# Sliding-window attention and an MLP mixer on one core: the float32 loads of q on ScalarE's DMA queue, with new order lists

## The chip, the core and the metric

The kernel runs on one core of a Trainium2 chip. The core has five engines that run side by side, each in its own program order: TensorE (PE, matrix multiplies), VectorE (DVE), ScalarE (ACT), GpSimd (POOL) and SyncE (SP, which here only issues DMAs). They tell each other what is done by semaphores. DMAs are issued by an engine and carried out by DMA engines. TensorE writes into PSUM banks, from which VectorE or ScalarE copy the result into SBUF.

The metric is the device time of one execution in microseconds (us). Lower is better.

## The reference

Attention with a window of 128 and a linear bias over 8 batches of 8 heads, then a mixer over tokens and over channels (batch 8, sequence 576, head size 64, model width 512, token width 256, channel width 1536):

```python
scores = (1/8) * q @ k^T                  # per batch and head, 576 x 576
rel = pos[:, None] - pos[None, :]
scores = where((0 <= rel) & (rel < 128), scores - slope[h] * |rel|, -1e9)
attn = softmax(scores)
x = (attn @ v)                            # to batch x 576 x 512
h = relu(x^T @ w_tok1) @ w_tok2
u = x + h^T
out = u + relu(u @ w_ch1) @ w_ch2
```

The inputs and the output are float32; the matrix multiplies are done in bfloat16.

## The kernel before

The 576 tokens of a batch are four blocks of 128 and a tail of 64. A batch passes through these steps, each a small function that emits instructions, and each with a short name in the order lists. The digit is a block or a pair of heads (hp); a mark ' means the next batch, '' the one after.

- Loads: `v` (values), `l` and `q` (k and q of a pair of heads, of batches 0 and 1), `qt` (their tails), `Lk`, `Lq` (k and q of batches 2 to 7), `LW` (`W1`, `W1t`, `W2` of the token mixer), `G0` to `G2` (the three column groups of `WC1`, one group for four `C`), `H0`, `H1` (the two halves of `WC2`). All of these are issued by GpSimd, which casts to bfloat16 on the way, except `l0`, `q0`, `l1`, `q1` of batch 0: these are float32 loads through SyncE's queue (`load_f32`), and `ck0`, `cq0`, `ck1`, `cq1` cast them, k on ScalarE and q on VectorE.
- Transposes of q and k: for batches 0 and 1 on TensorE (`A0` to `A3`, `AT` for the tail), with copies out of PSUM that the tuples `AQ_ACT` and `AK_DVE` give to ScalarE or VectorE; for later batches by DMA (`Zq`, `Zk`).
- Scores: `S<kb><j>` for key block kb and head group j, then exp on ScalarE, then a multiply by the mask on VectorE. Batch 0 adds its bias on TensorE, and its first two scores are halves (`s0`, `t0` and so on).
- Probabilities times values: `P0` to `P4`; for batch 0 by pairs of heads, `p0` to `p3`.
- Token mixer: `K0`, `K1` (first product and relu), `U0` to `U3` and `UT` (second product and the sum with x); for batch 0 `k0` to `k3` and `u0` to `u3`.
- Transposes of u: `X0` to `X3`; for batches 0 to 2 on TensorE, for batches 3 to 7 by DMA from `X0` and `X2` (`U_DMA`). For batch 0, `x0` to `x3`.
- Channel mixer: `C0` to `C11` (first product, relu into `r2`, on VectorE for the members of `DVE_RELU`, else on ScalarE), `D<c><part>` (second product of block c in three parts, sum, store). Two batches share the tail: `T0` to `T2` and `E0` to `E2`. `Y` transposes the tail of u by DMA.
- Others: `W1` to `W4` are so many matrix multiplies of zeros that keep TensorE busy; `I`, `J`, `B` make the identity, the distances and the bias; `O`, `e1`, `e2`, `ek`, `ex`, `FC` are memsets on GpSimd; `M`, `m` make the masks; `LC` copies a constant.

Five lists hold the order in which these names are emitted: `PROLOGUE` and `FIRST` for batch 0, `SECOND` for batch 1, `PERIOD` for each of batches 2 to 6, and `LAST` for batch 7. The order of a list is the program order on every engine at once, so it sets which work fills an engine while another result is awaited, and the order of each DMA queue. `PERIOD` works on `C`, `D` of its batch, on `P`, `K`, `U`, `X` of the next and on `S` of the one after.

PSUM holds two double banks for scores and `P` (`psS`, taken in turn by `S2`), three banks for nearly all else (`psM`, taken in turn by `M`), and one for tails and zeros (`psT`). A step that takes a bank waits until the bank's last content has been copied out. The taking in turn:

```python
def S2():
    t = psS[srot[0] % 2]
    srot[0] += 1
    return t
def M():
    t = psM[mrot[0] % 3]
    mrot[0] += 1
    return t
```

Other tuples: `U_ACT` (the sum of `u` by an identity multiply on TensorE and a copy on ScalarE; else the sum on VectorE), `X_DVE` and `x_DVE` (copies of `X` and `x` on VectorE), `k_DVE` (relu of `k` on VectorE), `SPLIT` and `S_M` (scores of batch 0 with two exps, and in `psM`).

Of the kernel before, what the change touches and what calls it, by code (L numbers as in the profile page):

```python
# [16 lines left out]
CH2_PARTS = 3  # L17
MASK_LATER = 1
U_DMA = (3, 4, 5, 6, 7)
U_ACT = (0, 1, 2, 3)  # L20
X_DVE = (0, 1, 2)
K_DVE = (0,)
PROLOGUE = """
W4 O J I W3 l0 B W3 ck0 q0 l1 q1 l23 FC cq0 W1 q23 v4 A0 qt v2 v0 W3 ck1 cq1 s1 A1 v1 S00 t1 S20
W2 A3 v3 LW A2 AT S11 l01' S30 q01' ek ex S21 M3 p0 l23' LC q23' G0 p1 M1 S01 k0 S31 u0 p2 M2 k1
p3 qt' G1 M0 A1' A0' m0 W2 A2' u1 v2' e1 A3' e2 v4' S00'
"""
FIRST = """
G2 v3' k3 v1' x0 v0' H1 m1 H0 k2 S20' x1 W2 AT' u3 u2 Lk'' Lq'' UT Zq'' x3 Zk'' x2 S10' Lk'''
S31' v0''' C5 v4'' S30' S01' v3'' v0'' C11 C8 C9 S21' S11' E2 C3 C10 C4 Lq''' v1'' v2'' P4' C1  # L30
C7 v4''' E0 C2 C6 P2' C0 P0' P3' D00 v2''' P1' D01 D02 K0' K1' D10 D11 U1' D12 Zq''' U2' X1' U3'
U0' Zk''' D20 D30 D21 E1 D31 X2' UT' D22 S00'' D32 T0' X0'
"""
SECOND = """
Lk''' X3 S31' S30' C8 C7 S20' v1'' C5 S11' S01' C9 v1''' C11 C2 v3'' T1 P0' C3 Lq''' C1 C4 S10'
S21' T2 C10 C0 C6 v0''' P4' v2''' P1' D00 v3''' D01 P3' P2' D02 K0' K1' S20'' S01'' D10 D11 D12
U1' UT' U0' U2' v4''' U3' X0' S21'' S11'' D20 D21 X3' S10'' S00'' E0 E1 D22 E2 X2' D30 X1' D31
D32 P0''
"""
PERIOD = """  # L40
C7 Zq'' C3 S30' S31' C8 Zk'' C11 C6 Y C1 T0 P2' P4' T1 C4 C2 Lk''' P1' C10 C9 T2 P3' C0 C5 K0'
S01'' S00'' K1' D00 v3''' v4''' D01 Lq''' D02 U2' U0' UT' U3' v1''' U1' P0'' D20 v2''' D21 D10
v0''' X2' X3' X1' X0' D22 S10'' S11'' D30 D11 D31 D12 E0 S20'' S21'' D32 E1 E2
"""
LAST = """
C3 C0 C2 C8 T0 C9 C1 C5 T2 C4 C6 Y C11 T1 C7 C10 D00 E0 E1 D01 D02 D10 D11 E2 D20 D12 D21 D30
D22 D31 D32
"""
VROW = 96
NPB = 9  # L50
SPLIT = (0, 1, 3, 5, 6)
S_M = (2, 4, 5, 6)
S_P = ()
Y_DMA = (3, 5, 7)
x_DVE = (1, 3)
k_DVE = ()
AK_DVE = (0, 1, 2, 4, 6, 7)
AQ_ACT = (1, 2, 3, 4, 5, 6, 7)
DVE_RELU = (4, 5, 7, 8, 10)


@with_exitstack
def kernel(
# [57 lines left out]
    qf0 = T("qf0", [P, 4, 4 * D], f32)  # L121
    kf0 = T("kf0", [P, 4, 4 * D], f32)
# [593 lines left out]
    def tok2_hp(hp):  # L716
        def f():
            t = M()
            hc = slice(hp * P, (hp + 1) * P)
            for c in range(NC):  # L720
                for j in range(2):
                    nc.tensor.matmul(t[:, c * P:(c + 1) * P], lhsT=W2[:, j, c * P:(c + 1) * P],
                                     rhs=r1[0][:, j, hc], start=(c == 0 and j == 0),
                                     stop=(c == NC - 1 and j == 1 and hp not in U_ACT))
# [87 lines left out]
    def fill_x1():  # L812
        nc.gpsimd.memset(xt[1][:, :], 0.0)

    def load_f32(dst, src, hp):
        hs = slice(2 * hp, 2 * hp + 2)
        nc.sync.dma_start(out=dst[:, hs, :],
                          in_=src[0, hs, 0:SM, :].rearrange("h (p j) d -> p h (j d)", j=4))

    def cast_f32(cp, dst, src, hp):  # L820
# [9 lines left out]
    def names(b):  # L830

        d = {}
        for kb in range(NC):
            for j in range(2):
                d[f"S{kb}{j}"] = score(b, kb, j)
        for qb in range(NC):
            d[f"P{qb}"] = pv(b, qb)
        d["P4"] = pv_tail(b)
        for i in range(2):
            d[f"K{i}"] = tok1(b, i)  # L840
        for c in range(NC):
            d[f"U{c}"] = tok2(b, c)
            d[f"X{c}"] = utrans(b, c)
        d["UT"] = tok2_tail(b)
        for ht in range(NHT):
            d[f"C{ht}"] = ch1(b, ht)
        if b % 2:
            for g in range(3):
                d[f"T{g}"] = ch1_tail(b, g)
            if b in Y_DMA:  # L850
                d["Y"] = utail_trans(b)
        for c in range(NC):
            for i, f in enumerate(ch2(b, c, CH2_PARTS)):
                d[f"D{c}{i}"] = f
        if b % 2:
            for i, f in enumerate(ch2_tail(b, CH2_PARTS)):
                d[f"E{i}"] = f
        for c in range(NC + 1):
            d[f"v{c}"] = lambda c=c: load_v(b, c)
        if b >= PE_BATCHES:  # L860
            d["Lq"], d["Lk"] = lambda: load_tokens(qn, qnt, q, b), lambda: load_tokens(kn, knt, k, b)
            d["Zq"] = lambda: dma_transpose(qT[b % 2], qn, qnt)
            d["Zk"] = lambda: dma_transpose(kT[b % 2], kn, knt)
        else:
            for nm, dst, src in (("q", qs, q), ("l", ks, k)):
                for hp in range(NHP):
                    d[f"{nm}{hp}"] = lambda dst=dst, src=src, hp=hp: load4(dst, src, b, hp)
                for hp in (0, 2):
                    d[f"{nm}{hp}{hp + 1}"] = lambda dst=dst, src=src, hp=hp: load4(dst, src, b, hp, 4)
            d["qt"] = lambda: load_qk_tail(b)  # L870
            for hp in range(NHP):
                d[f"A{hp}"] = pe_transpose(b, hp)
            d["AT"] = pe_transpose_tail(b)
        if b == 0:
            for hp in range(NHP):
                d[f"M{hp}"] = lambda hp=hp: mask_exps(hp)
                d[f"p{hp}"] = pv_hp(hp)
                d[f"k{hp}"] = tok1_hp(hp)
                d[f"u{hp}"] = tok2_hp(hp)
                d[f"x{hp}"] = utrans_hp(hp)  # L880
            for hp in range(2):
                d[f"q{hp}"] = lambda hp=hp: load_f32(qf0, q, hp)
                d[f"l{hp}"] = lambda hp=hp: load_f32(kf0, k, hp)
                d[f"cq{hp}"] = lambda hp=hp: cast_f32(nc.vector.tensor_copy, qs, qf0, hp)
                d[f"ck{hp}"] = lambda hp=hp: cast_f32(nc.scalar.copy, ks, kf0, hp)
            d["LC"] = late_constants
            d["FC"] = first_constants
            d["e1"], d["e2"] = lambda: ones_v(1), lambda: ones_v(2)
            d["ek"], d["ex"] = fill_k1, fill_x1
# [62 lines left out]
```

## Time and profile before

| | |
|---|---|
| median of 5 runs | 293.05 us (292.74 to 294.53) |
| the profiled execution | 292.99 us, of which its span is 290.9 us |
| granted TensorE clock | 1.00 in every stretch |
| instructions in the profile | 6132 |
| loads and stores | 38.38 MB, mean 132 GB/s |
| issues of the float32 loads, per load | 256 KB, 0.45 us on SyncE, 3.6 us (k) and 3.8 us (q) to landing |

How to read it: the span runs from the first to the last instruction; the profiled execution's time is a little longer. Busy time of an engine is the union of its instructions. TensorE's multiplies are pipelined, so that a row's duration (379 ns for 512 columns) is longer than its distance to the next (0.22 us). A chain of waits leads back from the last instruction, at each step to what released it. In the timeline a bracket holds the idle time ahead of an instruction and what ended it. SPq and POOLq are the sequencers' entries, in which a DMA is issued.

### The profile page before, as it was taken

To read this page: it belongs to the slowest core of one execution; us is meant where nothing else is said; L and a number is where in the kernel's file an instruction comes from. 1 tells how busy PE (TensorE), PEld (TensorE's weight loads), DVE (VectorE), ACT (ScalarE), POOL (GpSimd) and SP (SyncE) were. 2 spreads that over 40 slices of the span, in tenths; PEclk is the share of its full clock that TensorE was granted. 3 is DMA by queue.
4 is the path that set the end of the run, shared out by engine and by line. 5 is a ranking of instruction groups with operands and counts; after the bars stand their busy time and mean duration, and the time that the engine had idled before them with its cause. 6 is when DMAs were issued, how large, how long until landed. Compare 5 with 4: busy or idle time off the path is not lost.

```text
span 290.9 us, 6132 instructions
## 1 busy us (share of the span) xinstructions
PE 280.0 (96%) x2531; PEld 155.9 (54%) x2552; DVE 157.0 (54%) x310; ACT 124.9 (43%) x195; POOL 103.6 (36%) x140
## 2 busy tenths in 40 slices
PE   8898999999999999999999999998999999999995
PEld 3476646554574555544664455543664456545543
DVE  4246676547467557646637457646637467522222
ACT  3897962028715452326441552326441552104300
POOL 8996743079339605920294004920000000000000
PEclk9999999999999999999999999999999999999999
DMA  7999999799999999999899577999603620042014
GB/s 169 147 186 197 181 206 155 145 166 140 168 167 175 160 226 82 136 152 229 106 130 162 131 156 106 139 156 182 146 0 87 96 72 2 36 110 90 0 50 132
DMA packets 150267, 38.38 MB, mean 132 GB/s; under 512 B 137440, under 2 KB 145760, under 8 KB 150240
## 3 DMA queue, kind: packets, MB, share of 16 engines
q0 software_dynamic: 103152, 17.41, 79.0%
q1 hardware_dynamic: 47088, 20.59, 32.2%
q8 instruction: 20, 0.33, 0.5%
q14 instruction: 7, 0.06, 0.0%
HBM read 35.85 MB, written 9.44 MB: 156 GB/s over the span
## 4 chain that ended last, share of the span: by engine, by line
PE 84%; DMA 6%; POOL 5%; ACT 2%; issue 2%; DVE 1%; POOLq 0%; ACTq 0%
PE psM L548 29%; PE psM L607 25%; PE psM L481 4%; PE psM L506 4%; PE psT L565 4%; PE psM L629 4%; PE psS L356 3%; DMA utb<-ub 3%; DMA qs<-in_q_dram 3%; PE psS L420 2%; PE psS L416 2%; POOL vp L190 1%; PE psS L448 1%; ACT pe L370 1%; PE psM L588 1%
## 5 line engine op out<-in xcount | busy, mean ns | idle before, releaser
L548 PE MATMUL psM<-utb,WC 128*128 128x512 bf16 x384 | 89.4, 379 | 2.0 <-DMA utb<-ub 1.2
L607 PE MATMUL psM<-WC,r 128*128 128x512 bf16 x353 | 84.8, 379 | 0.9
L370 ACT ACTIVATE pe<-psS 128x1024 bf16<-128x1024 f32 x56 | 54.5, 1025 | 42.1 <-PE psS L356 41.8
L548 PEld LDWEIGHTS <-WC 128*128 128x128 bf16 x384 | 35.3, 98 | 41.0 <-issue 3.6
L554 ACT ACTIVATE r<-psM 128x512 bf16<-128x512 f32 x56 | 33.3, 599 | 54.5 <-PE psM L548 54.5
L607 PEld LDWEIGHTS <-r 128*128 128x128 bf16 x372 | 34.3, 98 | 40.8 <-issue 3.8
L190 POOL DMA_DIRECT2D kn<-in_k_dram x24 | 21.0, 889 | 76.8 <-DMA kT<-kn 75.5
L376 DVE TENSOR_TENSOR pb<-pe,masks 128x1024 bf16<-128x1024 bf16 x42 | 29.0, 690 | 27.2 <-ACT pe L370 27.2
L612 DVE TENSOR_TENSOR ob<-psM,ub 128x512 f32<-128x512 f32 x31 | 21.4, 690 | 28.3 <-PE psM L607 26.6
L551 DVE TENSOR_SCALAR r<-psM 128x512 bf16<-128x512 f32 x40 | 27.4, 688 | 16.2 <-PE psM L548 15.9
L190 POOL DMA_DIRECT2D vp<-in_v_dram x32 | 29.1, 947 | 1.8 <-DMA WC<-in_moe_w_ch_dram 1.6
L190 POOL DMA_DIRECT2D qn<-in_q_dram x24 | 21.3, 936 | 6.3 <-DMA WC<-in_moe_w_ch_dram 5.8
L430 DVE TENSOR_TENSOR xb<-psS,rt 128x512 bf16<-128x512 f32 x28 | 19.4, 692 | 1.0
L508 DVE TENSOR_TENSOR ub<-psM,xb 128x512 bf16<-128x512 f32 x28 | 17.5, 682 | 1.5 <-PE psM L506 1.5
L420 PE MATMUL psS<-vp,pb 128*128 128x65 bf16 x224 | 15.7, 193 | 0.0
L420 PEld LDWEIGHTS <-pb 128*128 128x128 bf16 x224 | 13.6, 97 | 3.1
L429 DVE RECIPROCAL rt<-psS 128x8 f32<-128x8 f32 x28 | 5.7, 204 | 17.0 <-PE psS L420 17.0
L506 PE MATMUL psM<-r,W 128*128 128x512 bf16 x56 | 14.5, 379 | 0.0
L356 PE MATMUL psS<-qT,kT 64*128 64x256 bf16 x168 | 13.3, 272 | 0.5 <-ACT pe L370 0.5
L481 PE MATMUL psM<-xb,W 128*128 128x256 bf16 x112 | 13.4, 273 | 0.0
L416 PE MATMUL psS<-vp,pb 128*128 128x65 bf16 x168 | 12.8, 193 | 0.0
L565 PEld LDWEIGHTS <-WC 128*128 128x128 bf16 x192 | 11.6, 98 | 2.3 <-issue 0.2
(131 smaller groups left out, 300.4 us busy)
## 6 DMA issues: line engine op xcount, KB each, us to landing
out_dram<-ob SPq DMA_DIRECT2D x31, 256.0 KB, 2.4
vp<-in_v_dram POOLq DMA_DIRECT2D x32, 128.0 KB, 5.6
kn<-in_k_dram POOLq DMA_DIRECT2D x24, 128.0 KB, 4.4
qn<-in_q_dram POOLq DMA_DIRECT2D x24, 128.0 KB, 4.8
WC<-in_moe_w_ch_dram POOLq DMA_DIRECT2D x3, 512.0 KB, 10.3
WC<-in_moe_w_ch_dram POOLq DMA_DIRECT2D x2, 768.0 KB, 12.6
out_dram<-ob SPq DMA_DIRECT2D x10, 128.0 KB, 2.4
ks<-in_k_dram POOLq DMA_DIRECT2D x3, 256.0 KB, 6.1
```

The costliest lines, as they stand in the source:

```text
L190: nc.gpsimd.dma_start(out=dst, in_=src[b, :, c * P:(c + 1) * P, :].rearrange("h s d -> s h d"))
L356: nc.tensor.matmul(s[h][:, a * 256:(a + 1) * 256], lhsT=kT[i][r, kb, hp, :], rhs=qT[i][r, kb:kb + 2, hp, :], start=True, stop=True)
L370: nc.scalar.activation(out=e[:, h, :], in_=s[n][:, None, :] if split else t2[:, :, :], func=ACT.Exp, scale=scale)
L376: nc.vector.tensor_tensor(out=p[:, :].rearrange("p (h x) -> p h x", h=2), in0=e[:, :, :], in1=masks[:, j].rearrange("p h g a x -> p h (g a ...
L420: nc.tensor.matmul(ov, lhsT=prob(b, qb, h, 0), rhs=vt[:, qb, h, 0:D + 1], start=first, stop=(hh == 3))
L481: nc.tensor.matmul(st["t"][h][:, dh * 256:(dh + 1) * 256], lhsT=W1[:, c, dh * P:(dh + 1) * P], rhs=by_half(xb[b % 2][:, c, :])[:, h], star ...
L506: nc.tensor.matmul(t[:, :], lhsT=W2[:, j, c * P:(c + 1) * P], rhs=r1[b % 2][:, j, :], start=(j == 0), stop=(j == 1))
L548: nc.tensor.matmul(t[:, :], lhsT=WC1[:, cb, ht * P:(ht + 1) * P], rhs=utb[b % 2][:, :, cb, :], start=(cb == 0), stop=(cb == NCB - 1))
L551: nc.vector.tensor_scalar(out=r2[b % 2][:, ht, :], in0=t[:, :], scalar1=0.0, scalar2=None, op0=ALU.max)
L554: nc.scalar.activation(out=r2[b % 2][:, ht, :], in_=t[:, :], func=ACT.Relu)
L565: nc.tensor.matmul(psT[:, j * P:(j + 1) * P], lhsT=WC1[:, cb, ht * P:(ht + 1) * P], rhs=utt[pi2][:, cb, :, :], start=(j == 0 and cb == 0), ...
L607: nc.tensor.matmul(t[:, :], lhsT=r2[b % 2][:, ht, c * P:(c + 1) * P], rhs=WC2[:, ht, :], start=(ht == 0), stop=(ht == NHT - 1))
```

## The change

`load_f32` gets the queue as an argument: q's two float32 loads are issued by ScalarE, k's two stay on SyncE. All five order lists are different, and eight tuples that say which engine copies what. No step is added or taken away; only u0 of batch 0, which leaves `U_ACT`, loses four identity multiplies on TensorE and is added on VectorE instead.

```diff
-U_ACT = (0, 1, 2, 3)
-X_DVE = (0, 1, 2)
+U_ACT = (1, 2, 3)
+X_DVE = (0, 2)
 PROLOGUE = """
-W4 O J I W3 l0 B W3 ck0 q0 l1 q1 l23 FC cq0 W1 q23 v4 A0 qt v2 v0 W3 ck1 cq1 s1 A1 v1 S00 t1 S20
-W2 A3 v3 LW A2 AT S11 l01' S30 q01' ek ex S21 M3 p0 l23' LC q23' G0 p1 M1 S01 k0 S31 u0 p2 M2 k1
-p3 qt' G1 M0 A1' A0' m0 W2 A2' u1 v2' e1 A3' e2 v4' S00'
+l0 q0 l1 q1 W4 I J W3 B O ck0 W3 l23 q23 FC W1 cq0 v4 qt A0 cq1 v0 v2 W3 ck1 s1 A1 S00 t1 v1 S20
+v3 W2 A2 A3 AT q01' S11 LW S30 l23' W2 ex ek l01' S21 p0 M1 q23' G0 LC p1 M2 S01 k0 S31 u0 p3 M3
+k1 p2 qt' G1 v4' M0 A1' A0' m1 u1 m0 A2' S10'
 """
 FIRST = """
-G2 v3' k3 v1' x0 v0' H1 m1 H0 k2 S20' x1 W2 AT' u3 u2 Lk'' Lq'' UT Zq'' x3 Zk'' x2 S10' Lk'''
-S31' v0''' C5 v4'' S30' S01' v3'' v0'' C11 C8 C9 S21' S11' E2 C3 C10 C4 Lq''' v1'' v2'' P4' C1
-C7 v4''' E0 C2 C6 P2' C0 P0' P3' D00 v2''' P1' D01 D02 K0' K1' D10 D11 U1' D12 Zq''' U2' X1' U3'
-U0' Zk''' D20 D30 D21 E1 D31 X2' UT' D22 S00'' D32 T0' X0'
+A3' v3' e2 k3 G2 v1' v2' v0' k2 x0 S00' H0 e1 H1 S20' AT' W2 u3 u2 UT Lk'' x1 Lq'' Zq'' x3 Zk''
+Lk''' v0''' x2 S30' v0'' C5 v3'' v1'' S01' E2 S31' C11 C8 C9 S21' S11' C3 C4 C10 Lq''' v2'' P4'
+C1 v4'' C7 C0 P2' C2 C6 v4''' P0' v2''' P3' D00 E0 D01 P1' D02 K0' K1' D10 D11 U1' D12 X1' Zq'''
+U3' U0' U2' D20 D21 D30 X2' UT' Zk''' D31 S00'' D22 S20'' D32 E1 T0' X0'
 """
 SECOND = """
-Lk''' X3 S31' S30' C8 C7 S20' v1'' C5 S11' S01' C9 v1''' C11 C2 v3'' T1 P0' C3 Lq''' C1 C4 S10'
-S21' T2 C10 C0 C6 v0''' P4' v2''' P1' D00 v3''' D01 P3' P2' D02 K0' K1' S20'' S01'' D10 D11 D12
-U1' UT' U0' U2' v4''' U3' X0' S21'' S11'' D20 D21 X3' S10'' S00'' E0 E1 D22 E2 X2' D30 X1' D31
-D32 P0''
+X3 S31' S30' C8 Lk''' v0''' C5 S01' T1 v2''' S11' C11 C7 C3 C6 P0' C4 S10' S21' v3'' v1''' C0 T2
+C9 v3''' C1 C10 P4' v1'' C2 P1' Lq''' D00 D01 P3' P2' D02 K0' K1' S20'' S01'' D10 D11 D12 U1'
+UT' U0' U2' v4''' U3' X0' S21'' S11'' D20 D21 X3' S00'' S10'' D22 E0 E1 E2 X2' D30 D31 X1' D32
+P0''
 """
 PERIOD = """
-C7 Zq'' C3 S30' S31' C8 Zk'' C11 C6 Y C1 T0 P2' P4' T1 C4 C2 Lk''' P1' C10 C9 T2 P3' C0 C5 K0'
-S01'' S00'' K1' D00 v3''' v4''' D01 Lq''' D02 U2' U0' UT' U3' v1''' U1' P0'' D20 v2''' D21 D10
-v0''' X2' X3' X1' X0' D22 S10'' S11'' D30 D11 D31 D12 E0 S20'' S21'' D32 E1 E2
+Zq'' C11 C3 C7 S31' S30' C8 Zk'' Y P2' C1 C6 C4 C9 C10 T0 P4' C0 P1' C2 Lk''' T1 P3' C5 T2 K0'
+K1' S01'' Lq''' v4''' S00'' D00 D01 D02 U2' U0' v3''' UT' U3' U1' v0''' v1''' P0'' D20 X1' v2'''
+D10 D21 X2' X0' D22 S10'' X3' S11'' D11 D30 D31 D12 E0 S21'' S20'' D32 E1 E2
 """
 LAST = """
-C3 C0 C2 C8 T0 C9 C1 C5 T2 C4 C6 Y C11 T1 C7 C10 D00 E0 E1 D01 D02 D10 D11 E2 D20 D12 D21 D30
-D22 D31 D32
+C10 C4 C5 T2 C2 C7 C8 C3 T0 C6 C11 T1 C0 C1 C9 D00 E0 D01 E1 Y D02 D10 D11 E2 D12 D30 D20 D31
+D21 D22 D32
 """
-SPLIT = (0, 1, 3, 5, 6)
+SPLIT = (1, 3, 4, 5)
-x_DVE = (1, 3)
-k_DVE = ()
-AK_DVE = (0, 1, 2, 4, 6, 7)
-AQ_ACT = (1, 2, 3, 4, 5, 6, 7)
-DVE_RELU = (4, 5, 7, 8, 10)
+x_DVE = (0, 1, 2)
+k_DVE = (1,)
+AK_DVE = (1, 2, 4, 6)
+AQ_ACT = (2, 4, 5, 6)
+DVE_RELU = (3, 5, 7, 10, 11)
...
-    def load_f32(dst, src, hp):
+    def load_f32(queue, dst, src, hp):
         hs = slice(2 * hp, 2 * hp + 2)
-        nc.sync.dma_start(out=dst[:, hs, :],
+        queue.dma_start(out=dst[:, hs, :],
                           in_=src[0, hs, 0:SM, :].rearrange("h (p j) d -> p h (j d)", j=4))
...
-                d[f"q{hp}"] = lambda hp=hp: load_f32(qf0, q, hp)
-                d[f"l{hp}"] = lambda hp=hp: load_f32(kf0, k, hp)
+                d[f"q{hp}"] = lambda hp=hp: load_f32(nc.scalar, qf0, q, hp)
+                d[f"l{hp}"] = lambda hp=hp: load_f32(nc.sync, kf0, k, hp)
```

## The prediction

> **What bounds the kernel now.** I read the page first, then the stretches of the span as a table, then what TensorE waits for in the first 36 us, then the chain of waits and the timelines around those waits. From the page:
>
> ```profile
> PE 280.0 (96%) x2531; PEld 155.9 (54%) x2552; DVE 157.0 (54%) x310; ACT 124.9 (43%) x195; POOL 103.6 (36%) x140
> PE 84%; DMA 6%; POOL 5%; ACT 2%; issue 2%; DVE 1%; POOLq 0%; ACTq 0%
> ```
>
> TensorE is busy for 280.0 of 290.9 us, and the chain lies on it for 84%. An order can only win back the 10.9 us in which it is idle. Where they are, by stretch (first number after the times: width, second: TensorE busy):
>
> ```profile
> 0.00:11.30 11.30, 9.76 (x73) 4.12 (x73) 3.87 (x16) 6.68 (x13) 10.25 (x24) 1.00 1.05 161
> 11.30:22.60 11.30, 10.48 (x206) 8.29 (x206) 5.08 (x15) 10.18 (x27) 11.20 (x18) 1.00 1.64 176
> 22.60:35.70 13.10, 11.46 (x202) 8.40 (x202) 7.83 (x21) 11.11 (x21) 8.72 (x13) 1.00 1.64 188
> ...
> 132.90:166.00 33.10, 32.74 (x297) 18.55 (x300) 18.37 (x35) 13.61 (x20) 12.57 (x15) 1.00 1.28 147
> 166.00:198.80 32.80, 31.51 (x255) 16.31 (x257) 20.56 (x38) 13.91 (x19) 12.57 (x15) 1.00 1.40 146
> 198.80:232.00 33.20, 33.07 (x299) 18.72 (x302) 17.76 (x34) 13.52 (x20) 0.00 (x0) 1.00 0.50 94
> 262.00:291.00 29.00, 25.34 (x164) 13.94 (x164) 7.23 (x12) 5.97 (x10) 0.00 (x0) 1.00 0.22 68
> ```
>
> The first 35.7 us hold 1.54 + 0.82 + 1.64 = 4.0 us of idle TensorE, the end 3.7 (its last result on the way out), the iterations between 0.1 to 1.3 each. In the first 35.7 us ScalarE is nearly full as well (10.18 of 11.30, 11.11 of 13.10). What TensorE waits for there (us, times, longest), and the chain at the same place (start, us):
>
> ```profile
> PE psM L234 <- DMA qs<-in_q_dram: 1.2, 2, 0.7
> PE psS L356 <- ACT pe L370: 0.5, 1, 0.5
> PE psM L234 <- ACT qT L239: 0.5, 2, 0.2
> PE psM L722 <- ACT r L713: 0.4, 1, 0.4
> 17.31 7.98 DMA qs<-in_q_dram
> ```
>
> Loads of q set the pace twice: at 11.30 (q23) and at 25.34 (q23', issued at 17.31). The queue's rate over the first 30 us, in 40 slices, levels off near 200 GB/s from 16 us on: the loads stand behind one another.
>
> ```profile
> GB/s 0 0 53 280 352 223 258 206 148 164 145 158 135 153 146 150 148 170 124 148 178 175 175 195 191 187 195 195 196 197 208 201 203 207 183 173 201 203 197 174
> ```
>
> Where the queue edit acts, in the timelines (start, us):
>
> ```profile
> 0.80 1.28 ACT L822 ACT_TABLE_LOAD   x1 [0.80 <-PEq L936]
> 1.33 0.45 SPq L817 DMA_DIRECT2D qf<-in_q_dram  x1
> 3.64 1.26 DVE L791 TENSOR_SCALAR sid<-ident 128x128 bf16<-128x128 bf16 x8 [0.22 <-POOL ident L776]
> 4.64 0.52 DVE L822 CAST qs<-qf 128x512 bf16<-128x512 f32 x1
> 1.06 4.61 PE L750 MATMUL psT<-zt 128*128 128x512 bf16 x11 [1.06 <-DVE zt L745]
> 5.60 0.41 PE L234 MATMUL psM<-ident,qs 128*64 128x128 bf16 x8
> ```
>
> The first cast of q starts when VectorE is through with `sid` (line 791), not when q lands, and TensorE is filled with 11 warm-up matmuls until about 5.5 us.
>
> **What the Trainium skill says.** "DMA: Bandwidth & Descriptors", section "Issuing engines are not separate DMA queues": loads issued from several engines run on the same 16 DMA engines and interleave; only the issuing time is saved. The trace agrees as far as it goes: one issue on SP takes 0.45 us, the rate afterwards is common to all. "ScalarE: Activation LUTs", "What ACT_TABLE_LOAD costs": the load proper takes 1283 ns; the trace has 1.28 us, and it now stands behind two issues. "TensorE: Matmul & The Clock Gate", "What's actually happening": the array starts at half clock and needs about 3.4 us of work. That fits the 11 warm-up matmuls, which fill 4.6 us and of which the change keeps all.
>
> **The change part by part.** Durations are those of the profiled execution: span 290.9, time 292.99, so 2.09 lie around the span; the median of the runs is 293.05, 0.06 more.
>
> 1. Queue of q. Two issues leave SP and go ahead of the table load on ScalarE: 2 x 0.45 = 0.9 us, so the table is in at about 0.80 + 0.9 + 1.28 = 3.0 us. The first cast of k on ScalarE starts at 3.70 and waited 1.6 us for its load: the issues are hidden. Without that cover they cost 0.9. q's first piece is issued at 0.8 in place of 1.33, but then shares the engines with k's, so I take the landing as unchanged to 0.5 earlier. I, J before O bring `ident` forward by over 1 us, so `sid` and the cast end sooner; next late is the warm-up: the last starts at 5.29 and takes 0.21, floor 5.50. Gain 0.1.
> 2. q23 is issued before FC (four memsets, 4.46 to 5.42): 0.94 us earlier. It can land 0 to 0.9 earlier, since the engines are busy; I take 0.4. The transposes A2, A3 start at 11.30 minus 0.45, floor 10.21 + 0.43 - 0.1 = 10.55.
> 3. Copies shifted by the tuples: VectorE instead of ScalarE for u0, the relu of k1, x0 and x2 (x3 to ScalarE), and two of the q copies of hp 3; one k copy goes back. Net four ScalarE instructions of about 0.59 less, 2.4 us in 10 to 35 us, and as much more on VectorE, which has 5.1 of 11.3 and 7.8 of 13.1 busy: cover enough. Without u0's four identity matmuls TensorE saves 4 x 0.056 = 0.2.
> 4. The loads reordered: before LW, l01', q01', l23', q23'; after q01', LW, l23', l01', q23'. A load of 256 KB takes 256 KB / 195 GB/s = 1.34 us of queue. The weights come 1.34 later: W2 landed at 13.53 + 5.5 = 19.0 (its issue, and the time to landing in the view of its tile, as for all landings here), now 19.0 + 1.34 - 0.4 = 19.95. u0 started at 20.18: no loss, but its floor. The transposes A1' started at 22.58 and need l01', now third: third place landed (l23', 16.58 + 8.0) at 24.58, of which 1.5 look like stragglers, as second place landed at 14.99 + 6.7 = 21.7 and 21.7 + 1.34 = 23.0. Less 0.4: between 22.6 and 24.2; I take 23.2, a loss of 0.6 there.
> 5. From A1' to C11. Before: 22.58 to 35.66, 13.1 us, in which the warm-up W2 is 0.43, the wait for q23' 0.89 (24.45 to 25.34) and ScalarE waits 0.27 + 0.24 + 0.67. After: W2 stands before S21, u1 lies under the wait for q23', and the score blocks are spread as S30' C5 S01' S31'. I take away 0.43, 0.89 and half of the 1.18, and give back 0.8 for u1 and A2', which now wait for the copies of A1' on ScalarE (0.5 each). 12.0 us. C11 begins at 23.2 + 12.0 = 35.2, 0.45 before the old 35.66. Floor: C11 needs G2, landed at 24.83 + 10.3 = 35.1, less 0.4.
> 6. FIRST and SECOND, 36 to 99 us: the wait of 0.5 at 56 us, where X1' needs the bank of D12, goes over to U3', which takes that bank now. Nothing.
> 7. PERIOD, five times 33 us. Zq'' moves ahead of two C, S01'' and S00'' behind K1', Lq''' together with Lk''', and other relus go to VectorE. SP's sequence of stores and transposes is the same instruction for instruction, POOL's the same loads in another order, and as many changes between full and half array (93 against 92). Between the transposes X0' and the next C lies the same work, so the waits of 0.85 (132 us) and 1.3 (197 us) for `utb` stay. Nothing, bounds -0.2 to +0.4 an iteration.
> 8. LAST: another order of the same C; the last two pieces, D22 and D32, are as before. Nothing.
>
> Sum: -0.45, span 290.45, time 292.5.
>
> **The rivals.** *Loads first.* Both halves of q and k land 0.9 sooner, l01' is in at 22.6, C11 reaches its floor near 34.7 (-0.95), and half of the 2.2 us of `utb` waits goes because the iterations' loads drain sooner: 292.99 - 0.95 - 1.1 = 290.9. For it: 4.0 us are there to be had. Against it: the rate in the stretch of loads is flat. *l01' late.* It lands at 24.6 with the stragglers: C11 at 36.6, +0.95: 293.9. For it: that place in the queue did so before. *P2' too early (the slower side).* In PERIOD, P2' now comes right after C8; before, C8, C11, C6 and C1 stood between. It takes the score bank of S31', whose exp lasts 1.03 and starts about 0.2 after the matmuls, while only S30' (0.54) and C8 (0.86) lie between: a margin of 0.2 us. It decides once ScalarE starts that exp more than 0.2 late; at 0.4 a time, five iterations, +2.0: 295.0. Against it: C11, C3, C7 ahead of it all have their relu on VectorE. *No effect*: the edits shift waits within the load-bound start; that is my forecast with -0.45 as a size.
>
> **How the numbers follow.** This measurement can tell about 0.5% (1.46 us) from no change. Forecast 292.5, chance 0.45; loads first 290.9, 0.24; l01' late 293.9, 0.14; P2' 295.0, 0.17. Faster by over 0.5% (under 291.6): most of the second and a little of the first, 0.27. Slower (over 294.5): most of the last and some of the third, 0.22. Rest 0.51. The range from 290.9 to 294.8 leaves out the further half of the two outer cases. The forecast's own range is 291.7 to 293.4.
>
> **What would show it.** Right: A2 at 10.6 to 11.1; A1' waiting for `ks` and starting at 22.6 to 24.2; no wait for `qs` at A2'; C11 at 34.8 to 35.7; the iterations at 33.1 on average; both `utb` waits still there. Wrong: TensorE waiting for ScalarE or VectorE at P2' (line 416) in every iteration; W1 or W2 awaited at k0 or u0; the iterations' `utb` waits gone or doubled.

## The result, and the profile after

| | before | after |
|---|---|---|
| median of all runs | 294.13 us (80 runs) | 293.49 us (43 runs) |
| ratio after / before, run side by side | | 0.9961, 95% [0.9945, 0.9978] |
| the profiled execution | 292.99 us, span 290.9 | 293.13 us, span 291.1 |

The change makes the kernel faster by 0.39%, between 0.22 and 0.55%; of the 293.05 us that stand for before ahead of the prediction, that is 1.1 us (0.6 to 1.6). The ratio leaves out executions that fell into a slower state, while the medians are over all of them, so that their quotient, 0.998, is another number. The forecast was 0.45 us, within 0.5%: the right side, and a little under the measured range. The two profiled executions do not show the gain: the one of after is even 0.14 us longer, and the one of before is among the shorter ones (15 of its 80 are shorter still). So the first question is where a gain sits that one pair of traces hides.

The page of after (busy time by engine, the chain, and the queue that is new):

```profile
PE 280.6 (96%) x2527; PEld 155.8 (54%) x2548; DVE 158.7 (55%) x312; ACT 124.7 (43%) x192; POOL 103.3 (35%) x140
PE 82%; DMA 9%; POOL 5%; issue 1%; ACT 1%; DVE 1%; POOLq 0%; ACTq 0%
q10 hardware_dynamic: 544, 0.52, 0.5%
```

TensorE runs four instructions less (u0's identity multiplies), ScalarE three less, VectorE two more. The chain now lies more on DMA (9% for 6%). The stretches, cut at the same events as those of before (A2; A1'; C11; then the same times):

```profile
0.00:10.52 10.52, 9.46 (x72) 4.07 (x72) 4.08 (x16) 6.11 (x11) 9.51 (x23) 1.00 1.09 174
10.52:23.13 12.61, 10.98 (x203) 8.16 (x202) 6.05 (x17) 10.15 (x26) 11.65 (x18) 1.00 1.51 164
23.13:34.85 11.72, 11.21 (x201) 8.68 (x199) 8.49 (x23) 10.13 (x18) 8.41 (x13) 1.00 1.60 191
...
132.90:166.00 33.10, 32.97 (x298) 18.62 (x301) 18.33 (x34) 13.45 (x20) 12.58 (x15) 1.00 1.29 146
166.00:198.80 32.80, 31.43 (x255) 16.23 (x255) 20.89 (x39) 13.78 (x19) 12.58 (x15) 1.00 1.36 147
198.80:232.00 33.20, 33.05 (x298) 18.65 (x301) 17.91 (x34) 13.47 (x20) 0.00 (x0) 1.00 0.42 90
262.00:291.00 29.00, 25.51 (x165) 14.04 (x164) 7.40 (x12) 5.97 (x10) 0.00 (x0) 1.00 0.23 69
```

The way to C11 is 34.85 us long instead of 35.7: the first stretch is 0.8 shorter, the second 1.3 longer, the third 1.4 shorter. From 132.9 us on, TensorE's busy time is that of before within 0.3 us. What TensorE waits for in the first 36 us (us, times, longest), and the chain there (start, us):

```profile
PE psM L704 <- DMA W<-in_moe_w_tok_dram: 1.2, 1, 1.2
...
PE psM L548 <- DMA WC<-in_moe_w_ch_dram: 0.2, 1, 0.2
```

```profile
12.16 6.71 DMA W<-in_moe_w_tok_dram
...
24.02 10.79 DMA WC<-in_moe_w_ch_dram
...
34.85 2.76 PE psM L548 x12
```

Both waits for q (1.2 us before) and the waits for ScalarE are gone. In their place stands one wait for the first half of the token weights (k0, line 704), which landed at 12.16 + 6.71 = 18.87 us, and a short one for the last column group of `WC1` (C11, line 548).

How far the work has come in the two traces, in us from the start of the span:

| | A0 | A2 | k0 | A1' | C11 | first C of batch 2 | of batch 3 | of batch 5 | of batch 7 | last result of TensorE |
|---|---|---|---|---|---|---|---|---|---|---|
| before | 5.60 | 11.30 | 18.28 | 22.58 | 35.66 | 102.76 | 133.16 | 198.83 | 261.26 | 287.45 |
| after | 5.39 | 10.52 | 18.91 | 23.13 | 34.85 | 102.33 | 132.92 | 198.84 | 261.43 | 287.61 |

The lead of 0.8 us at C11 is 0.4 at 102 us, 0.2 at 133 and gone at 199. Two things take it: the lists behind C11, and two waits for `utb`, the transposed u, near 132 and 197 us.

The lists first. In the 14 traces of this case (before, after and the twelve experiments below) the way between milestones depends on the list alone, to 0.02 us, once the two waits are taken off:

| us | old list (5 traces) | new list (9 traces) |
|---|---|---|
| C11 to the first C of batch 2 (`FIRST`, `SECOND`) | 67.11 | 67.48 |
| first C of batch 2 to that of batch 7, less the two waits (`PERIOD`, five times) | 156.34 | 156.72 |
| first C of batch 7 to the last result of TensorE (`LAST`) | 26.18 | 26.18 |

So the new lists give back 0.37 + 0.38 = 0.75 us of what the start gains. In `FIRST`, 0.11 of it is a longer wait for a bank (0.46 us at U3' for 0.35 at X1'); the rest there was not traced. In `PERIOD` the cause can be seen at P2' (line 416), which now stands right behind C8 (line 548) and takes the score bank that the exp of S31' (line 370) still reads. First after, then before, where more C stand between (start, us):

```profile
136.05 1.94 ACT L370 ACTIVATE pe<-psS 128x1024 bf16<-128x1024 f32 x2 [3.08 <-PE psS L365]
136.17 1.04 PE L548 MATMUL psM<-utb,WC 128*128 128x512 bf16 x4
137.12 0.19 PE L416 MATMUL psS<-vp,pb 128*128 128x65 bf16 x1
```

```profile
141.74 1.89 PE L548 MATMUL psM<-utb,WC 128*128 128x512 bf16 x8
143.46 0.19 PE L416 MATMUL psS<-vp,pb 128*128 128x65 bf16 x1
```

At their usual distance of 0.216 us the four matmuls of C8 make room for P2' at 137.03; it starts at 137.12, 0.05 after the first of the two exps is through (136.05 + 1.02). In before it starts as soon as the matmuls ahead of it make room (141.74 + 8 x 0.215). The same 0.08 us stands in each of the five iterations of all nine traces with the new `PERIOD`, each time 51 to 52 ns behind the end of that exp, and in none with the old one: 0.4 us in five. In the list of waits it is missing, since that counts idle time from the modelled end of the matmul before, which lies later than its turn.

Then the waits. In after they are the two for `utb` that before has:

```profile
PE psM L548 <- DMA utb<-ub: 1.2, 1, 1.2
PE psM L548 <- DVE pb L376: 0.8, 1, 0.8
```

The second is put down to VectorE, which had long been done; the second transpose of u, issued at 124.7 us and 8.1 on its way, landed at 132.8, and C started at 132.9. Counted as the gap less the usual distance of two matmuls, the two waits are 0.97 and 1.41 us in after, 0.85 and 1.32 in before, 0.2 us more. With that the account of the pair closes: -0.81 at C11, +0.37, +0.38 and +0.21 make +0.15, and the last result comes at 287.61 for 287.45. Such a wait ends with a transfer, not with TensorE. The issues of the transfers for 132 us followed TensorE's lead (123.3 and 124.7 us in after, 123.6 and 125.0 in before), but their time on the way, 7.8 to 8.7 us, differs by more than the lead. So a lead that TensorE brings there can be lost or can grow.

### The profile page after: what moved, and what is told of

It is laid out like the page before. It is cut to its first block, busy times and chain, and to the rows that moved or that the text cites. A ratio compares the mean times of both kernels' runs of the same rounds, so it can differ in the third digit from the quotient of the medians.

```text
span 291.1 us, 6139 instructions
## 1 busy us (share of the span) xinstructions
PE 280.6 (96%) x2527; PEld 155.8 (54%) x2548; DVE 158.7 (55%) x312; ACT 124.7 (43%) x192; POOL 103.3 (35%) x140
## 4 chain that ended last, share of the span: by engine, by line
PE 82%; DMA 9%; POOL 5%; issue 1%; ACT 1%; DVE 1%; POOLq 0%; ACTq 0%
PE psM L548 29%; PE psM L607 25%; PE psM L506 4%; PE psM L481 4%; PE psT L565 4%; DMA WC<-in_moe_w_ch_dram 4%; PE psM L629 4%; DMA utb<-ub 3%; PE psS L356 3%; PE psS L420 2%; DMA W<-in_moe_w_tok_dram 2%; PE psS L416 2%; POOL vp L190 1%; PE psS L448 1%; POOL qkt L193 1%
## 5 line engine op out<-in xcount | busy, mean ns | idle before, releaser
L554 ACT ACTIVATE r<-psM 128x512 bf16<-128x512 f32 x56 | 33.5, 599 | 36.6 <-PE psM L548 36.6
L499 ACT ACTIVATE r<-psM 128x512 bf16<-128x512 f32 x7 | 4.2, 598 | 22.4 <-PE psM L490 22.4
```

The source lines that it names most:

```text
L554: nc.scalar.activation(out=r2[b % 2][:, ht, :], in_=t[:, :], func=ACT.Relu)
```

## The experiments

Each ratio is to the kernel before, run side by side on the same chip, with its 95% interval. The runs e1 to e4, e5 to e8 and e9 to e12 are of three chips, on which before had medians of 293.09, 294.07 and 293.21 us, so medians are compared within such a group only. "C11" and "waits" (the two for `utb`, near 132 and 197 us) are of the profiled execution.

### The queue and the parts

**e1_queue_alone**: before, with q on ScalarE's queue and the four loads at the head of the list (`load_f32` takes the queue as in the change; "..." marks what is left out).

```diff
-W4 O J I W3 l0 B W3 ck0 q0 l1 q1 l23 FC cq0 W1 q23 v4 A0 qt v2 v0 W3 ck1 cq1 s1 A1 v1 S00 t1 S20
+l0 q0 l1 q1 W4 O J I W3 B W3 ck0 l23 FC cq0 W1 q23 v4 A0 qt v2 v0 W3 ck1 cq1 s1 A1 v1 S00 t1 S20
...
-                d[f"q{hp}"] = lambda hp=hp: load_f32(qf0, q, hp)
+                d[f"q{hp}"] = lambda hp=hp: load_f32(nc.scalar, qf0, q, hp)
```

> The kernel before with nothing changed but the queue: the four float32 loads are issued first, q's on ScalarE and k's on SyncE; all else in the old order. If the gain (about 0.4%, 1.1 us) comes from the start's order, this gives 0 to 0.3 us less than before: the first transposes at 5.4 to 5.5 in place of 5.60, q23 still awaited until about 11.0 to 11.3. If the second queue is the cause, it gives about 1 us less than before, with q23 in before 10.6.

Measured: 0.9987 [0.9962, 1.0012]; C11 35.22; waits 0.62 and 1.37. A2 came at 11.41 us, no earlier than in before, though q23 was in at 10.77. The middle of the ratio is 0.4 us less; the "about 1 us" of a queue that is the cause lies at the end of the interval.

**e2_queue_undone**: after, with q back on SyncE's queue.

```diff
-                d[f"q{hp}"] = lambda hp=hp: load_f32(nc.scalar, qf0, q, hp)
+                d[f"q{hp}"] = lambda hp=hp: load_f32(nc.sync, qf0, q, hp)
```

> The changed kernel with all four float32 loads on SyncE's queue again, in the order k, q, k, q. If the order of the start is the cause, it stays within 0.3 us of the changed kernel, with A2 at 10.5 to 10.9 and k0 waiting for W1 until about 19. If the second queue is the cause, it falls back to the time of the kernel before.

Measured: 0.9971 [0.9946, 0.9995]; C11 34.54; waits 1.46 and 1.36. C11 comes as early as with two queues, so the lists bring it forward without the second queue. At 102 us this run led before by 0.73 us; at 133.10 by 0.06, after a wait for `utb` of 1.46.

**e3_start_alone** and **e4_period_alone**: e3 is after with the `PERIOD`, the `LAST` and (from batch 2 on) the relu tuple of before; e4 is before with those of after.

```diff
...
-            if ht in DVE_RELU:
+            if ht in (DVE_RELU if b < 2 else DVE_RELU_LATER):
```

> The changed kernel's PROLOGUE, FIRST, SECOND and tuples with the old PERIOD and LAST (and the old relu engines from batch 2 on). If the start is the cause: ratio to before about 0.996, as the whole change; the first C of batch 1's successors (102.8 before) about 0.4 sooner. If the new PERIOD is the cause: 1.000.

Measured: 0.9990 [0.9965, 1.0015]; C11 34.55; waits 1.00 and 0.57. The first C of batch 2 came at 102.03, 0.73 us sooner than in before, and still the ratio is not the 0.996 expected of a start that is the cause.

> The old PROLOGUE, FIRST, SECOND and tuples with the changed PERIOD and LAST (and the new relu engines from batch 2 on). If the start is the cause: ratio 1.000, within 0.1%. If the new PERIOD is the cause: about 0.996, with the waits for the transposed u at 132 and 197 us shorter than 0.85 and 1.3. If P2' right after C8 costs a wait, slower than before by up to 0.4 an iteration.

Measured: 0.9993 [0.9969, 1.0017]; C11 35.61; waits 0 and 1.47.

What follows from the four: all lists together without the queue (e2) are faster than before, by 0.05 to 0.54%; the queue, the start and the period alone can't be told from nothing. The start moves C11 forward in e2 and e3, the new period (e4) doesn't, and the waits for `utb` are between 0 and 1.5 us whatever the lists. The two parts, 0.1% each at their middle, don't add up to 0.39%, but their intervals are wide enough for it.

### Where the start now waits

**e5_weights_first**: after, with the token weights ahead of q01' and l01' ahead of l23', the order of the loads in before.

```diff
-v3 W2 A2 A3 AT q01' S11 LW S30 l23' W2 ex ek l01' S21 p0 M1 q23' G0 LC p1 M2 S01 k0 S31 u0 p3 M3
+v3 W2 A2 A3 AT LW S11 q01' S30 l01' W2 ex ek l23' S21 p0 M1 q23' G0 LC p1 M2 S01 k0 S31 u0 p3 M3
```

> The changed kernel with the loads of batch 1 and the token mixer's weights in an order near the old one (LW, q01', l01', l23', q23'). Theory: the wait of 1.3 us for W1 ahead of k0 goes (k0 at about 17.6, A1' at about 22.0), but C11 still needs G2, whose place in the queue is the same, so it starts at 34.5 to 34.8 as in the changed kernel (34.85) and the time stays within 0.3 us of it. Rival: the wait for W1 is what limits the start; then C11 comes about 1 us sooner, at 33.9, and the time falls by as much.

Measured: 0.9968 [0.9945, 0.9991]; k0 at 17.73 for 18.91, A1' at 21.86 for 23.13, C11 at 35.37 for 34.85; waits for `utb` 0.30 and 1.73. What TensorE waits for in the first 36 us of this run:

```profile
PE psM L548 <- DMA WC<-in_moe_w_ch_dram: 1.3, 1, 1.3
...
PE psM L234 <- DMA qs<-in_q_dram: 0.8, 1, 0.8
PE psM L722 <- DMA W<-in_moe_w_tok_dram: 0.4, 1, 0.4
```

The wait at k0 goes and A1' follows it 1.3 us forward. What the wait at k0 alone was worth, e5 doesn't tell: in after l01' landed at 23.31 us and A1' took it up at 23.38, so without the wait at k0 A1' would have met that load, and e5 moved both forward. Then the time is waited for again: for q23', and for the last group of `WC1`. C11 came 0.5 us later than in after, where it was expected as early or up to 0.35 earlier, and the ratio is that of after within the intervals. The start is bound by the loads in a row; here the load moved forward handed the wait to the next.

### The two waits for u

In before and in after the loads of a batch (k, q, v by GpSimd) begin when the DMA transposes of q and k have freed their source. They then still run when SyncE issues the transposes of u at the end of the iteration. **e6_z_early** takes after and issues `Zq`, `Zk` one stage earlier, behind D22 (in `SECOND` behind X2') instead of at the head of the next iteration; `Lq` of batch 4 goes right behind its `Lk`.

```diff
-X3 S31' S30' C8 Lk''' v0''' C5 S01' T1 v2''' S11' C11 C7 C3 C6 P0' C4 S10' S21' v3'' v1''' C0 T2
+X3 S31' S30' C8 Lk''' Lq''' v0''' C5 S01' T1 v2''' S11' C11 C7 C3 C6 P0' C4 S10' S21' v3'' v1''' C0 T2
-C9 v3''' C1 C10 P4' v1'' C2 P1' Lq''' D00 D01 P3' P2' D02 K0' K1' S20'' S01'' D10 D11 D12 U1'
+C9 v3''' C1 C10 P4' v1'' C2 P1' D00 D01 P3' P2' D02 K0' K1' S20'' S01'' D10 D11 D12 U1'
-UT' U0' U2' v4''' U3' X0' S21'' S11'' D20 D21 X3' S00'' S10'' D22 E0 E1 E2 X2' D30 D31 X1' D32
+UT' U0' U2' v4''' U3' X0' S21'' S11'' D20 D21 X3' S00'' S10'' D22 E0 E1 E2 X2' Zq''' Zk''' D30 D31 X1' D32
-Zq'' C11 C3 C7 S31' S30' C8 Zk'' Y P2' C1 C6 C4 C9 C10 T0 P4' C0 P1' C2 Lk''' T1 P3' C5 T2 K0'
+C11 C3 C7 S31' S30' C8 Y P2' C1 C6 C4 C9 C10 T0 P4' C0 P1' C2 Lk''' T1 P3' C5 T2 K0'
-D10 D21 X2' X0' D22 S10'' X3' S11'' D11 D30 D31 D12 E0 S21'' S20'' D32 E1 E2
+D10 D21 X2' X0' D22 Zq''' Zk''' S10'' X3' S11'' D11 D30 D31 D12 E0 S21'' S20'' D32 E1 E2
```

> The changed kernel with the DMA transposes of q and k (Zq, Zk) of batches 4 to 7 issued one stage earlier (after E2 in SECOND, after D22 in PERIOD), and Lq of batch 4 right after its Lk. Theory: the two waits for the transposed u (about 1.0 at 132 us and 1.4 at 197 us) come from loads that are still draining under those transposes, and they swallow what the start gains. With the loads released 3 to 6 us sooner the wait at 197 goes to under 0.4 and the one at 132 to under 0.5: 1.2 to 2.4 us less than before's ratio of 0.996, thus 0.988 to 0.992. Rival: the waits are the transposes' own length (3 to 4 us each) or the early transposes block SP's stores: no gain, or slower with TensorE waiting for the stores' buffers.

Measured: 0.9924 [0.9895, 0.9954], median 291.15 (expected were 0.988 to 0.992); no wait for `utb` in the profiled execution. GpSimd's timeline, after and then e6 (start, us, then the load of k of batch 7; in the bracket how long GpSimd was idle before, and what ended it):

```profile
178.56 3.50 POOL L190 DMA_DIRECT2D kn<-in_k_dram  x4 [22.84 <-DMA kT<-kn]
```

```profile
167.67 3.51 POOL L190 DMA_DIRECT2D kn<-in_k_dram  x4 [17.81 <-DMA kT<-kn]
```

GpSimd waits for the transpose `kT<-kn` both times; in e6 that ends 10.9 us sooner. The two transposes of u that end near 197 us, after and then e6, by the view of the tile (ns to issue; then us from issue to landing):

```profile
L528 SPq DMA_TRANSPOSE utb<-ub x2: 1233/2126/3019, 188.8 to 190.1; - x2
...
DMA to landing us min/median/max: 7.1/7.9/8.6
```

```profile
L528 SPq DMA_TRANSPOSE utb<-ub x2: 1259/1273/1287, 188.0 to 189.3; - x2
...
DMA to landing us min/median/max: 3.1/3.2/3.3
```

The same two transposes take 7.9 us in after and 3.2 in e6. In after the loads were still landing until 198.5 us; in e6 the last was in at 183.9. The stretches of e6 that end at those two C (width, TensorE busy first):

```profile
132.10:166.00 33.90, 33.79 (x303) 18.96 (x304) 19.45 (x36) 15.22 (x22) 12.57 (x15) 1.00 1.36 160
166.00:196.60 30.60, 30.44 (x251) 15.97 (x253) 19.07 (x36) 11.94 (x17) 12.57 (x15) 1.00 1.25 145
```

TensorE is idle for 0.16 us in the second, where after had 1.37.

This reaches the second wait only. At 132 us the loads were still landing in e6 too, until 130.4 us (after: 132.2), and the transposes of u took 7.1 and 5.8 us there (after: 8.7 and 8.1); that TensorE did not wait for them can be chance, as e4, without early transposes, hardly waited there either. Over all traces the wait at 197 us is 0 in the seven with early transposes and 0.6 to 1.7 in the seven others; the wait at 132 us is 0 to 1.2 in the former and 0 to 1.5 in the latter.

**e8_old_z_early** makes the same change to the kernel before (the lines of `SECOND` are left out here).

```diff
...
-C7 Zq'' C3 S30' S31' C8 Zk'' C11 C6 Y C1 T0 P2' P4' T1 C4 C2 Lk''' P1' C10 C9 T2 P3' C0 C5 K0'
+C7 C3 S30' S31' C8 C11 C6 Y C1 T0 P2' P4' T1 C4 C2 Lk''' P1' C10 C9 T2 P3' C0 C5 K0'
-v0''' X2' X3' X1' X0' D22 S10'' S11'' D30 D11 D31 D12 E0 S20'' S21'' D32 E1 E2
+v0''' X2' X3' X1' X0' D22 Zq''' Zk''' S10'' S11'' D30 D11 D31 D12 E0 S20'' S21'' D32 E1 E2
```

> The kernel before with the same early transposes of q and k. Theory: the waits at 132 and 197 us go here as well (1.2 to 2.2 us less than before, ratio 0.993 to 0.996), and with them gone in both kernels the changed start shows in full: e6 lies 0.4 to 0.8 us below this one. Rival: the changed start is worth nothing by itself; then e6 and this one agree within 0.2 us.

Measured: 0.9922 [0.9895, 0.9950], median 291.09; waits 0.30 and 0; last result of TensorE at 285.71 us (e6: 285.40). The gain does not need the change under study: it is larger than that of the change, the old lists have it as well, and with it the old and the new lists can't be told apart. The 0.4 to 0.8 us that e6 was to lie below this run did not come. That fits the account above: of 0.77 us at C11 (35.79 and 35.02) the new lists give back 0.75.

**e7_both**: e5 and e6 together.

> e5 and e6 together. Theory: the same as e6 within 0.3 us, since the weights' order is not what binds. Rival: 1 us less than e6.

Measured: 0.9930 [0.9908, 0.9953], no wait for `utb`, but C11 only at 36.18, with 1.4 us of waiting for q23' and 1.1 for `WC1`. To put the weights first buys nothing here either: the median, 291.69, is 0.5 us above that of e6.

### The group of WC1 that C11 needs

C5 takes the second column group of `WC1`, C11 the third, and the first is not needed until C3. **e9_groups_swapped** (from e6), **e10_old_groups_swapped** (from e8) and **e11_weights_and_groups** (from e7) load the second group first, then the third, then the first. The edit in e9 (in the other two the same three names):

```diff
-v3 W2 A2 A3 AT q01' S11 LW S30 l23' W2 ex ek l01' S21 p0 M1 q23' G0 LC p1 M2 S01 k0 S31 u0 p3 M3
-k1 p2 qt' G1 v4' M0 A1' A0' m1 u1 m0 A2' S10'
+v3 W2 A2 A3 AT q01' S11 LW S30 l23' W2 ex ek l01' S21 p0 M1 q23' G1 LC p1 M2 S01 k0 S31 u0 p3 M3
+k1 p2 qt' G2 v4' M0 A1' A0' m1 u1 m0 A2' S10'
-A3' v3' e2 k3 G2 v1' v2' v0' k2 x0 S00' H0 e1 H1 S20' AT' W2 u3 u2 UT Lk'' x1 Lq'' Zq'' x3 Zk''
+A3' v3' e2 k3 G0 v1' v2' v0' k2 x0 S00' H0 e1 H1 S20' AT' W2 u3 u2 UT Lk'' x1 Lq'' Zq'' x3 Zk''
```

> e6 with the three column groups of WC1 loaded in the order in which C needs them: G1 (C5), G2 (C11, C8, C9), then G0 (C3). Theory: C11 waits for G2 (0.2 to 1.4 us in the changed kernel and its variants), so the wait goes, C11 starts at about 34.3 and the first C of batch 1 0.3 to 0.7 sooner than in e6; time 0.3 to 0.7 us below e6, ratio to before about 0.990. Rival: the wait moves to C3 for G0, or to another load, at no gain.

Measured: 0.9927 [0.9899, 0.9956], median 290.98; C11 at 34.26 (e6: 35.02), no wait for `WC1`; a wait of 0.7 for `utb` near 132 us, where TensorE now comes earlier than the transfer. C11 came forward as expected; the 0.3 to 0.7 us less than e6 do not show in the ratios (0.9927 and 0.9924).

> The kernel before with early transposes of q and k (e8) and the same order of WC1's groups. Theory: its C11 starts later (35.7 before) and waited only 0.3 for G2, so it gains at most 0.3 over e8; with neither the transposed u nor G2 in the way, the changed start lies 0.5 to 1.0 us below the old one (e9 below this). Rival: the starts are worth the same; e9 and this agree within 0.2 us and their first C of batch 2 (102 us) too.

Measured: 0.9943 [0.9926, 0.9959], median 291.63; C11 at 35.77 as in e8 (35.79); a wait of 1.2 for `utb` near 132 us. With the old lists the group is not what C11 waits for. The median of e9 is 0.65 us lower, as expected; the intervals of the two overlap.

> e9 with the token mixer's weights ahead of q01' (as in e5). Theory: k0 no longer waits (17.8 in place of 18.7), but A2' then waits for q23', which is last in the queue in both; C11 at about 34.3 as in e9, time within 0.3 us of it. Rival: the wait for W1 was worth 1 us once G2 is out of the way.

Measured: 0.9915 [0.9892, 0.9938], median 290.51, the lowest of its group; its interval lies below that of after. In its profiled execution there is no wait left for `WC1`, for the token weights, or over 0.3 us for `utb`; the largest one in the start is for q23':

```profile
PE psM L234 <- DMA qs<-in_q_dram: 1.5, 1, 1.5
```

Against e9 it wins 0.5 us by the medians, more than the 0.3 expected and less than the 1 us of the rival. Against e10, the old lists with the same two remedies and nearly the same order of batch 1's loads, it wins 1.1 us (290.51 and 291.63), clear of the scatter: about 0.5 us to either side, an estimate from the spread of the 6 and 21 executions that their ratios count. In the traces its C11 is 1.50 us ahead (34.27 and 35.77), the lists give back 0.75, and it waits 0.95 us less for `utb` at 132 us; so part of the lead is the lists, and part a wait that differs from execution to execution.

**e12_queue_undone_clean**: e9 with q on SyncE's queue (the diff of e2).

> e9 with all four float32 loads on SyncE again. Theory: the queue is worth 0 to 0.3 us (first transposes 0 to 0.2 later, A2 0 to 0.4 later, hidden by the wait for W1): within 0.3 us of e9. Rival: with the later waits gone the queue shows its worth: 0.5 us or more above e9.

Measured: 0.9937 [0.9914, 0.9961], median 290.90; C11 at 34.94 for 34.26. Three pairs now compare the queue alone: before with e1 (-0.13%), e2 with after (-0.10%), e12 with e9 (-0.10%). By these ratios all point the same way, but by the medians of e9 and e12 on their chip (290.98 and 290.90) it is the other way. None is resolved; the one that isolates the queue against before, e1, leaves room for a gain of 0.38% at most. What the queue does move is q23: with the new lists it landed at 9.1 to 10.0 us with two queues (seven traces) and at 10.7 and 11.3 us with one (e2, e12), issued at the same time.

### How steady the start is

Four runs each of kernels with the same start let one see what of the 0.8 us repeats. (In e9 and e10 the groups of `WC1` are in another order; that doesn't touch A0 and A2.)

| us | A0 | A2 | C11 |
|---|---|---|---|
| new start: after, e3, e6, e9 | 5.39, 5.24, 5.86, 5.10 | 10.52, 10.37, 11.42, 10.24 | 34.85, 34.55, 35.02, 34.26 |
| old start: before, e4, e8, e10 | 5.60, 5.20, 5.61, 5.79 | 11.30, 11.91, 11.04, 10.92 | 35.66, 35.61, 35.79, 35.77 |

A0 overlaps, A2 overlaps, C11 doesn't: without e9 and e10 its means are 34.81 and 35.69. The runs with the queue the other way round agree: C11 is at 34.54 (e2) and 34.94 (e12) with the new lists and at 35.22 (e1) with the old ones. So the lists move C11. What the queue adds is open: with it C11 is 0.44 earlier in e1 and 0.68 in e9, but 0.31 later in after. And the lead hangs on the order of the loads: with the weights first it shrinks or goes (35.37 in e5, 36.18 in e7) unless the groups of `WC1` are put in order too (34.27 in e11). What moves A0 is the duration of the eleven warm-up matmuls ahead of it, here in after, e6 and e11 (start, us), whose starts are alike:

```profile
1.06 4.40 PE L750 MATMUL psT<-zt 128*128 128x512 bf16 x11 [1.06 <-DVE zt L745]
```

```profile
1.06 4.88 PE L750 MATMUL psT<-zt 128*128 128x512 bf16 x11 [1.06 <-DVE zt L745]
```

```profile
1.06 3.89 PE L750 MATMUL psT<-zt 128*128 128x512 bf16 x11 [1.06 <-DVE zt L745]
```

The Trainium skill, "TensorE: Matmul & The Clock Gate", section "What you observe", puts the change to full clock at around 4 us of sustained matmuls, give or take 500 ns from run to run. The trace agrees: over all runs the eleven took 3.89 to 4.88 us, with the same instructions; the distance of two starts falls from 427 to 216 ns from the eighth on in e11, from the tenth on in after, and not within the eleven in e6. In all but e5, A0 starts within 0.1 us of their end.

## Why the prediction was right, and where it was not

The forecast "within 0.5%, a little faster" holds, and the start came forward as it said, by twice the size. Behind the start two steps that it put at nothing cost 0.75 us. By its steps:

**1. Queue of q:** *gain 0.1, the issues hidden, table in at 3.0.* The issues are hidden. The timeline of after (start, us, idle before):

```profile
0.80 1.03 ACTq L817 DMA_DIRECT2D qf<-in_q_dram  x2
1.87 1.28 ACT L822 ACT_TABLE_LOAD   x1 [1.87 <-issue]
2.95 1.42 DVE L791 TENSOR_SCALAR sid<-ident 128x128 bf16<-128x128 bf16 x8
4.23 0.62 ACT L822 CAST ks<-kf 128x512 bf16<-128x512 f32 x1 [1.08 <-DMA kf<-in_k_dram]
4.56 0.43 DVE L822 CAST qs<-qf 128x512 bf16<-128x512 f32 x1 [0.19 <-DMA qf<-in_q_dram]
```

Table in at 3.15, 1.1 us ahead of k's data. But "landing unchanged to 0.5 earlier" was wrong: issued together, the first pieces land later. From issue to landing, shortest first, q before and then after:

```profile
L817 SPq DMA_DIRECT2D qf<-in_q_dram x2: 454/462/469, 1.3 to 2.3; - x2
...
DMA to landing us min/median/max: 3.0/3.8/4.5
```

```profile
L817 ACTq DMA_DIRECT2D qf<-in_q_dram x2: 476/503/530, 0.8 to 1.3; - x2
...
DMA to landing us min/median/max: 3.7/4.2/4.6
```

q's first piece was in at 1.33 + 3.0 = 4.3 us before and is at 0.8 + 3.7 = 4.5 after; k's first cast went from 3.70 to 4.23. Only the second pieces win (k 6.17 to 5.59, q 6.86 to 5.95). That is what the prediction cites from "DMA: Bandwidth & Descriptors", "Issuing engines are not separate DMA queues" (they interleave on the same engines), with its price in this trace. The 0.2 us of A0 in this pair is within what the warm-up does by itself.

**2. q23 earlier:** *A2 at 10.85, 0.45 gained.* 10.52 in the pair, but runs of the same start reach from 10.24 to 11.42. The mean of four is 10.64 against 11.29, 0.65: right in kind, and no single trace could have given the size. The 0.4 for the landing was too small in this pair: q23 was in at 9.28 for 11.26, A2 no longer waited for it and stood at its floor (10.55).

**3. Copies shifted:** *covered.* No wait for ScalarE or VectorE over 0.2 us is left in the start but that for the first zeros, which both kernels have.

**4. Loads reordered:** *W2 in at 19.95, no loss at u0; A1' at 23.2 for want of l01', 0.6 lost.* A1' came at 23.13, for another reason. The term that failed is the delay of the weights: "1.34 later less 0.4". In before W1 took 5.5 us from its issue at 11.7 and was in at 17.2; in after it was in at 18.87, 1.7 later; W2 came at 20.59, not 19.95, just ahead of u0 at 20.63. And W1 is needed by k0, which stood at 18.28 and on which the step set no floor: k0 waited 1.2 us, and A1' stands behind it. With the weights first (e5), k0 and A1' both come 1.2 to 1.3 earlier. For l01' the step was right: it landed at 23.31, and A1' took it up at 23.38, so that it would have held A1' up had k0 not done so.

**5. From A1' to C11:** *12.0 us; C11 at 35.2, floor 34.7.* It took 11.72, and C11 came at 34.85, 0.2 us behind its floor, with the wait for `WC1` that the floor names. e6 and e9 confirm the floor: 0.6 us of wait there, and C11 0.76 earlier without it, 0.15 of which e9 had won by A1' (22.86 for 23.01).

**6. FIRST and SECOND:** *the 0.5 us goes from X1' to U3'.* It did (line 506, 0.46 at 56 us; line 538, 0.35, before). But "nothing" was wrong: from C11 to the first C of batch 2 the new lists take 67.48 us for 67.11.

**7. PERIOD:** *nothing; both waits stay.* They stay: 0.97 and 1.41. But five iterations take 156.72 us for 156.34, 0.08 each, inside the bounds of -0.2 to +0.4 and not nothing. It is the rival "P2' too early", right as a mechanism and at a fifth of its size: line 416 waits for the exp in every iteration, as that rival and one of the signs of being wrong have it, but for 0.08 us and not 0.4. The time of e4, -0.07% with an interval of 0.24% to both sides, can't show so little.

**8. LAST:** *nothing.* From the first C of batch 7 to the last result of TensorE: 26.18 us in both.

The sum. In the traces it is -0.9 us at C11 in the mean (-0.45 was forecast), +0.37 and +0.38 behind it (nothing was forecast) and nothing at the end: about -0.15 us, 0.05% of the time. The steps that failed are 4 (the weights), 6 and 7; two errors in opposite directions keep the sum small. That the measured 1.1 us (0.6 to 1.6) lies near the forecast is in part luck: neither the steps nor the traces account for most of it. The waits for `utb` don't either, as far as they were traced: their sum is 2.4, 2.8, 1.6 and 2.0 us in after, e2, e3 and e5, and 2.2, 2.0 and 1.5 in before, e1 and e4. Where the wait at 197 us is gone, the new lists lead the old ones by nothing in one pair (e6, 0.9924; e8, 0.9922), by 0.16% in the next (e9, 0.9927; e10, 0.9943), where C11 is 1.5 us ahead, and by 0.28% in the last (e11, 0.9915; e10). So where the 0.39% comes from stays open. What is shown: C11 is earlier by 0.9 us in the mean, by the lists and with the loads in the order of after, and with one queue as with two; the new lists themselves give back 0.75 us of it, in every trace that has them all; and the waits at 132 and 197 us, 0 to 1.7 us each, decide in a single execution what is left.

"Loads first" was the rival nearest to the start (C11 34.7); its second half, that the `utb` waits shrink as loads drain sooner, did not come with this change. It was right as a mechanism for the wait at 197 us: e6 and e8 make the loads of the later batches drain sooner, and that wait (1.3 us in before) is gone in all seven traces that do. They win 0.76 and 0.78%, about 2.3 us; the other 1 us is not accounted for, since the wait at 132 us is not tied to it. The executions also scatter less: a standard deviation of 0.6 to 0.8 us in e6 to e8, 1.0 in before and e5 on the same chip.

## What to carry to other kernels

A gain ahead of a point where the compute engine waits for a transfer is not safe yet: find the next such wait, and ask what sets the transfer's start and what else is on the DMA engines while it runs. Split the span at fixed milestones and take these waits off: what a list costs then repeated to 0.02 us here, while whole executions scatter by 1 us. A start that is late by less than the wait list can see (P2', 0.08 us) shows in the distance of two starts. When loads in a row bound a start, price a reorder at every consumer of each load that moves back, its first use and not only its last. And compare milestones over several executions: one trace told 0.2 us apart at A0 that the warm-up alone moves by nearly 1.

## What the runs showed of the hardware

- A DMA transpose of u from SBUF to SBUF took 3.1 to 3.3 us at 188 to 194 us in the seven traces with no load in flight there, and 5.8 to 8.9 us near 132 and 197 us wherever loads were still landing; then its issue on SyncE took up to 3.8 us as well, instead of 1.3. A few later ones took up to 4.9 us with no load in flight.
- Two queues with two 256 KB loads each, started together, gave the first pieces 0.5 (k) to 0.7 us (q) more from issue to landing than one queue with the same four loads: 3.3 to 3.4 and 3.7 to 3.8 us in eight traces, 2.7 to 2.9 and 3.0 to 3.1 in the six others.
- The eleven warm-up matmuls differ by 1.0 us between executions of the same instructions (3.89 to 4.88), and A0 with them.
- With its waits for transfers taken off, TensorE's way through five iterations took the same time in every execution traced, to 0.01 us: 156.34 with one list, 156.72 to 156.73 with the other.
